# Copying a chunk's four accumulators out of PSUM first and adding them one unit later, with the weight decoding moved behind

## The chip, the cores and the metric

One core of a Trainium2 chip runs the whole kernel. The metric is the device time of one execution in microseconds, given as the median of several runs. TensorE (PE) multiplies matrices, VectorE (DVE) and ScalarE (ACT) do elementwise work, SyncE (SP) issues the transfers. TensorE writes its sums to PSUM, whose banks of 128 x 512 float32 VectorE and ScalarE read.

## The reference

Three stages follow one another, with two batches of 3008 tokens and a width of 256:

```python
scores = matmul(z, z.T) / S              # z: 3008 x 64 for each batch
x = u * matmul(maximum(scores, 0)**2, v) # v: 3008 x 256
h = x @ w_in;  y = (h - tanh(h)) @ w_out                       # 2048 wide
out = (sigmoid(y @ w_gate) * (y @ w_val)) @ w_out2             # 1536 wide
```

The weights arrive as float64 and are decoded on the chip.

## The kernel before

**Units.** The tokens are cut into twelve chunks: six for each batch, five of 512 tokens and one of 448. The work on a chunk is a row of units. In the attention of the first eleven chunks (`HalfAttention`) a unit is a pair of key tiles, and there are 12 units to a chunk. For the last chunk (`Attention`) the units are mixed with those of the first feed-forward stage (`Ffn1`), and the second stage (`Ffn2`) follows in the same list.

**A unit's steps.** `front` (line 294) lets TensorE compute the scores of two key tiles into PSUM. `mid1` (line 306) lets ScalarE apply relu (line 310) and square (line 311), and then VectorE split the result into a rounded part `ah` (line 314) and a remainder `al` (line 315, which the profile shows under the helper's line 79). `back` (line 317) multiplies both parts with the values `v` and adds to the chunk's accumulators. Each accumulator is a PSUM bank. `HalfAttention` uses all four banks at once, `acc[h][d]`: h is the half of the rows of a key tile that two matmuls side by side work on, d the half of the 256 columns. The sum over h is the result.

**Order.** The order on every engine is written out by hand in one loop (lines 527 to 555). Iteration n first runs what `todo[n]` holds, then `front` and `mid1` of unit n, then `end` of a chunk that was finished one iteration earlier (`LATE = 1`), and then `back` of unit n - 2. Each engine has one queue and takes its instructions in this order. So VectorE has from the end of a unit's scores to that unit's `back`, two iterations later, to make `ah` and `al`, and what lies ahead in its queue uses up that time.

**What todo holds.** The steps that decode the weights, six iterations for a part of 512 columns or rows (lines 133 to 178): `magnitude`, `sign`, `join`, `rest(0)`, `rest(1)`, `add` on lines 155 to 177, nearly all VectorE's; the splits of `v`, `z`, `x` and of the decoded weights; and the loads.

**A chunk's turn.** In iteration n in which `back` of a chunk's last unit is issued (unit n is then the second of the next chunk) the loop runs `todo[n]`, `front`, `back`, and then `empty` (line 339): for each d ScalarE copies `acc[1][d]` to SBUF (line 344) and VectorE adds `acc[0][d]` from PSUM to it (line 345). `mid1` of unit n comes after that. The next chunk's first `back`, one iteration later, writes the same four banks, and so can't start before they have been read. In iteration n + 1 `end` (line 347) lets VectorE multiply the sum by `u` (line 349) and SyncE write the product to memory (line 350). There are eleven such turns in a run.

**Buffers.** `mid1` and `empty` take their SBUF tiles from a ring of nine (`work`, line 67), `u`, `v`, `z` and weights from a ring of 42 (`ring`, line 66).

Of the kernel before, what the change touches and what calls it, by code (L numbers as in the profile page):

```python
# [7 lines left out]
F32 = mybir.dt.float32  # L8
# [4 lines left out]
ALU = mybir.AluOpType  # L13

P = 128
NQ = 512
# [14 lines left out]
def squared_relu_attention__then__two_ffns(  # L31
# [17 lines left out]
    nc = tc.nc  # L49
# [4 lines left out]
    ND = D // P  # L54
# [20 lines left out]
    def tmp(shape, dtype, name):  # L75
        return work.tile([P, *shape], dtype, tag="w", name=name)
# [165 lines left out]
    class Attention(Unit):  # L242
# [41 lines left out]
        def end(self, acc):  # L284
            u, n = u_t[self.c], self.n
            for d in range(ND):
                nc.vector.tensor_tensor(out=u[:, d, :n], in0=acc[d][:, :n], in1=u[:, d, :n], op=ALU.mult)
            nc.sync.dma_start(out=spill[self.c], in_=u[:, :, :n])

    class HalfAttention(Attention):  # L290
# [47 lines left out]

        def empty(self, acc):
            n = self.n  # L340
            self.sum = tmp([ND, NQ], F32, "sum")
            for d in range(ND):
                t = self.sum[:, d, :n]
                nc.scalar.copy(t, acc[1][d][:, :n])
                nc.vector.tensor_tensor(out=t, in0=acc[0][d][:, :n], in1=t, op=ALU.add)  # L345

        def end(self, acc):
            u, n = u_t[self.c], self.n
            nc.vector.tensor_tensor(out=u[:, :, :n], in0=self.sum[:, :, :n], in1=u[:, :, :n], op=ALU.mult)
            nc.sync.dma_start(out=spill[self.c], in_=u[:, :, :n])  # L350

    class Ffn1(Unit):
# [92 lines left out]
    units = [HalfAttention(c, i) for c in range(NC - 1) for i in range(KP)]  # L445
# [12 lines left out]
    todo = {}  # L458
# [5 lines left out]
    for b in range(B):  # L464
# [14 lines left out]
        for j in range(NZ):  # L479
            n = need[j] + early[j]  # L480
# [3 lines left out]
    for c in range(NC):  # L484
        at(start[0, c] + 2, lambda c=c: load_u(c))
        n = start[1, c]
# [7 lines left out]
    n = 8  # L494
    half = start[0, NZ]
    split = {}
    for k, p in enumerate(parts):
# [5 lines left out]
        if half - 14 < n < half + 4:  # L503
            n = half + 4
    for f in range(N1):
        n = where[1, 0, f]
        at(n - 3, split["wi1_", f // 2][f % 2])
        at(n - 2, split["wo1_", f // 2][f % 2])
    for f in range(N2 // 2):
        n = where[1, 0, 0] + W2_LAG + 2 * f  # L510
# [7 lines left out]
    with tc.manual_schedule():  # L518
        nc.vector.memset(square_max, -SQUARE_MAX)
        nc.scalar.activation(warm, square_max, AF.Tanh)  # L520
        accs = {}
        backs = {}
        for n, u in enumerate(units):
            backs.setdefault(n + u.ahead, []).append(u)
        pending = []
        total = len(units)
        for n in range(total + 8):
            for fn in todo.pop(n, ()):
                fn()
            if n < total:  # L530
                units[n].front()
            ready = backs.pop(n, ())

            turn = any(u.last and isinstance(u, HalfAttention) for u in ready)
            if n < total and not turn:
                units[n].mid1()
            if 0 <= n - 1 < total:
                units[n - 1].mid2()
            if pending and n >= pending[0][0]:
                _, u, a = pending.pop(0)  # L540
                u.end(a)
            for u in ready:
                halves = isinstance(u, HalfAttention)
                if u.first:
                    accs[u.kind] = [
                        [psa.tile([P, NQ], F32, tag=f"acc{d}", name=f"acc{d}") for d in range(ND)] for _ in range(1 + halves)
                    ]
                acc = accs[u.kind] if halves else accs[u.kind][0]
                u.back(acc)
                if u.last:  # L550
                    if halves:
                        u.empty(acc)
                    pending.append((n + LATE, u, acc))
            if n < total and turn:
                units[n].mid1()
        assert not todo and not pending


# [26 lines left out]
```

## Time and profile before

| | us |
|---|---|
| median of 3 runs (1593.74 to 1595.03) | 1593.95 |
| the profiled execution's own time | 1595.15 |
| its span | 1593.4 |
| TensorE busy in it | 1578.7 (99%) |
| VectorE busy | 1110.1 (70%) |
| ScalarE busy | 1044.2 (66%) |

The eleven chunks of `HalfAttention` take the first 459 us of the span, some 40 us for each. The granted clock of TensorE is 1.0, its full 2.4 GHz, in all 40 slices. In a timeline a row gives start, duration and engine, the line of the kernel, the operation with its output and inputs, the count and, in brackets, how long the engine sat idle before it and what ended that. Instructions on one engine overlap by some tenths of a microsecond, so what one of them costs its queue is read from start to start.

### The profile page before, as it was taken

What the parts mean: (1) busy time and instruction counts of PE and PEld (TensorE: products, weight loads), DVE (VectorE), ACT (ScalarE), POOL (GpSimd) and SP (SyncE); (2) the same over time, 40 slices, a digit from 0 to 9 for tenths busy, and PEclk for the clock granted to TensorE, in tenths of its full rate; (3) what the DMA queues carried; (4) which work ended last, traced back from release to release, by engine and by line L of the source; (5) the groups of instructions that cost most, each with busy time, mean ns of one, the idle gap of its engine ahead of it and who ended that gap; (6) DMA issues with size and microseconds to landing.
All of it is one profiled execution on the core that took longest, in us unless ns stands there. A gap on an engine that the chain in (4) does not pass through costs nothing.

```text
span 1593.4 us, 21476 instructions
## 1 busy us (share of the span) xinstructions
PE 1578.7 (99%) x8980; PEld 1338.8 (84%) x8980; DVE 1110.1 (70%) x1256; ACT 1044.2 (66%) x1254; POOL 0.2 (0%) x4
## 2 busy tenths in 40 slices
PE   8999999999999999999999999999999999999999
PEld 6888889888888878888888888888888888888888
DVE  7988898988879886666656656666656566665542
ACT  8766678677678986666566656566656666666532
POOL 0000000000000000000000000000000000000000
PEclk9999999999999999999999999999999999999999
DMA  6222233211100000000000000000000000000000
GB/s 225 80 80 80 74 104 100 81 67 54 52 14 14 1 25 1 27 1 1 27 1 25 0 27 1 27 0 1 26 0 27 1 27 1 0 25 1 14 1 25
DMA packets 28161, 53.28 MB, mean 33 GB/s; under 512 B 1952, under 2 KB 10144, under 8 KB 28064
## 3 DMA queue, kind: packets, MB, share of 16 engines
q1 hardware_dynamic: 28064, 51.91, 9.5%
q8 instruction: 70, 1.15, 0.3%
q14 instruction: 27, 0.22, 0.0%
HBM read 39.58 MB, written 12.32 MB: 33 GB/s over the span
## 4 chain that ended last, share of the span: by engine, by line
PE 95%; DVE 2%; ACT 1%; DMA 1%; issue 1%; SPq 0%; DVEq 0%
PE acc L223 30%; PE gv L235 24%; PE acc L331 20%; PE h L235 16%; PE s L302 5%; PE s L257 1%; DMA vraw<-v 0%; DMA raw_wg<-w_gate 0%; DVE ah L314 0%; ACT a L310 0%; DVE e L79 0%; DVE v L79 0%; ACT a L311 0%; DVE al L79 0%; DVE th L378 0%
## 5 line engine op out<-in xcount | busy, mean ns | idle before, releaser
L79 DVE TENSOR_TENSOR e<-h,th 128x1024 f32<-128x1024 f32 (+1 forms) x96 | 115.5, 1203 | 285.1 <-ACT sq L373 285.1
L331 PE MATMUL acc<-ah,v 64*128 64x512 f32 (+1 forms) x2068 | 301.1, 387 | 1.8 <-DVE sum L345 1.7
L331 PEld LDWEIGHTS acc<-ah,v 64*128 64x128 f32 x2068 | 218.1, 185 | 33.8 <-DVE sum L345 2.9
L372 ACT ACTIVATE th<-h 128x1024 f32<-128x1024 f32 (+1 forms) x96 | 97.0, 1010 | 216.3 <-PE h L235 216.3
L235 PE MATMUL h<-xh,wi 128*128 128x512 f32 (+1 forms) x768 | 233.8, 386 | 0.8 <-DVE e L79 0.8
L223 PE MATMUL acc<-p,wo 128*128 128x512 f32 (+1 forms) x864 | 215.4, 385 | 0.0
L223 PE MATMUL acc<-gh,wo 128*128 128x512 f32 (+1 forms) x768 | 204.8, 386 | 0.5 <-DVE yl L79 0.4
L310 ACT ACTIVATE a<-s 128x1024 f32<-128x1024 f32 (+1 forms) x132 | 134.2, 1017 | 87.2 <-PE s L302 85.9
L223 PEld LDWEIGHTS acc<-p,wo 128*128 128x128 f32 x864 | 162.2, 188 | 30.0
L422 ACT ACTIVATE sg<-gv 128x512 f32<-128x512 f32 (+1 forms) x144 | 84.6, 588 | 156.8 <-PE gv L235 156.8
L331 PE MATMUL acc<-al,v 64*128 64x512 f32 (+1 forms) x1034 | 184.0, 388 | 0.1
L79 DVE TENSOR_TENSOR al<-a,ah 128x1024 fp32r<-128x1024 f32 (+2 forms) x145 | 173.4, 1196 | 7.4 <-DVE ah L314 0.5
L235 PE MATMUL gv<-yh,wg 128*128 128x512 f32 (+1 forms) x576 | 175.2, 385 | 0.0
L235 PE MATMUL gv<-yh,wv 128*128 128x512 f32 (+1 forms) x576 | 175.0, 385 | 0.0
L423 DVE TENSOR_TENSOR sg<-gv,sg 128x512 f32<-128x512 f32 (+1 forms) x144 | 98.0, 680 | 106.5 <-ACT sg L422 106.5
L235 PEld LDWEIGHTS h<-xh,wi 128*128 128x128 f32 x768 | 144.1, 188 | 28.1 <-DVE e L79 1.3
L223 PEld LDWEIGHTS acc<-gh,wo 128*128 128x128 f32 x768 | 144.1, 188 | 28.1 <-DVE yl L79 1.2
L235 PE MATMUL h<-xl,wi 128*128 128x512 f32 (+1 forms) x384 | 147.9, 385 | 0.0
L311 ACT ACTIVATE a<-a 128x1024 f32<-128x1024 f32 (+1 forms) x132 | 139.0, 1053 | 4.2
L378 DVE COPY_PREDICATED th<-m,e 128x1024 f32<-128x1024 uint32 (+1 forms) x96 | 131.4, 1369 | 10.3 <-ACT wv L183 0.5
L331 PEld LDWEIGHTS acc<-al,v 64*128 64x128 f32 x1034 | 114.2, 185 | 17.7 <-DVE al L79 3.3
L235 PEld LDWEIGHTS gv<-yh,wg 128*128 128x128 f32 x576 | 108.1, 188 | 20.2
(95 smaller groups left out, 2269.6 us busy)
## 6 DMA issues: line engine op xcount, KB each, us to landing
raw_wo<-w_out SPq DMA_DIRECT2D x14, 512.0 KB, 5.4
vraw<-v SPq DMA_DIRECT2D x10, 512.0 KB, 7.1
u<-uT SPq DMA_DIRECT2D x10, 512.0 KB, 7.3
x<-u SPq DMA_DIRECT2D x10, 512.0 KB, 3.1
xl<-x SPq DMA_DIRECT2D x10, 512.0 KB, 3.6
outT<-o SPq DMA_DIRECT2D x20, 256.0 KB, 2.1
raw_wi<-w_in SPq DMA_DIRECT2D x8, 512.0 KB, 8.3
zraw<-zT SPq DMA_DIRECT2D x12, 256.0 KB, 6.7
```

The costliest lines, as they stand in the source:

```text
L79: nc.vector.tensor_tensor(out=out, in0=a, in1=b, op=ALU.subtract)
L223: nc.tensor.matmul(acc[d][:, :n], wt[:, wi, w, d * P : (d + 1) * P], hl[ai], start=first and m == 0, stop=last and m == len(passes) - 1,)
L235: nc.tensor.matmul(ps, w[:, wi, d, fi * P : (fi + 1) * P], xs[xi][:, d, :n], start=m == 0, stop=m == len(passes) - 1)
L257: nc.tensor.matmul(self.ps[:, e, :n], k, z_t[b, self.j][:, h, :n], start=h == 0, stop=h == 1)
L302: nc.tensor.matmul(self.ps[:, e, :n], z_t[b, i // 4][r, ki ^ e, c : c + P], q[r, qi ^ e, :n], start=m == 0, stop=m == 2)
L310: nc.scalar.activation(s, self.ps[:, :, :n], AF.Relu, scale=SCALE)
L311: nc.scalar.activation(s, s, AF.Square)
L331: nc.tensor.matmul(acc[h][d][:, :n], vt[r, w, e, d * P : (d + 1) * P], self.hl[a][r, e, :n], start=self.first and banks[k] not in banks[:k ...
L372: nc.scalar.activation(t, h, AF.Tanh)
L378: nc.vector.copy_predicated(t, m.bitcast(U32), e)
L422: nc.scalar.activation(s[:, :n], self.ps[:, 0, :n], AF.Sigmoid)
L423: nc.vector.tensor_tensor(out=s[:, :n], in0=self.ps[:, 1, :n], in1=s[:, :n], op=ALU.mult)
```

## The change

`empty` now reads each bank once and adds nothing: for each d VectorE copies `acc[0][d]` and ScalarE copies `acc[1][d]`, to two tiles of their own. `end`, one iteration later, lets VectorE add the two tiles, in one instruction over both d, and then multiply by `u`. In a turn's iteration `todo[n]` runs last, behind `mid1` of unit n, where it ran first.

```diff
         def empty(self, acc):
             n = self.n
-            self.sum = tmp([ND, NQ], F32, "sum")
+            self.sums = [tmp([ND, NQ], F32, "sum") for _ in range(2)]
             for d in range(ND):
-                t = self.sum[:, d, :n]
-                nc.scalar.copy(t, acc[1][d][:, :n])
-                nc.vector.tensor_tensor(out=t, in0=acc[0][d][:, :n], in1=t, op=ALU.add)
+                nc.vector.tensor_copy(self.sums[0][:, d, :n], acc[0][d][:, :n])
+                nc.scalar.copy(self.sums[1][:, d, :n], acc[1][d][:, :n])
 
         def end(self, acc):
             u, n = u_t[self.c], self.n
-            nc.vector.tensor_tensor(out=u[:, :, :n], in0=self.sum[:, :, :n], in1=u[:, :, :n], op=ALU.mult)
+            s, t = (a[:, :, :n] for a in self.sums)
+            nc.vector.tensor_tensor(out=s, in0=s, in1=t, op=ALU.add)
+            nc.vector.tensor_tensor(out=u[:, :, :n], in0=s, in1=u[:, :, :n], op=ALU.mult)
             nc.sync.dma_start(out=spill[self.c], in_=u[:, :, :n])
...
         for n in range(total + 8):
-            for fn in todo.pop(n, ()):
-                fn()
+            ready = backs.pop(n, ())
+
+            turn = any(u.last and isinstance(u, HalfAttention) for u in ready)
+            if not turn:
+                for fn in todo.pop(n, ()):
+                    fn()
             if n < total:
                 units[n].front()
...
-            if n < total and turn:
-                units[n].mid1()
+            if turn:
+                if n < total:
+                    units[n].mid1()
+                for fn in todo.pop(n, ()):
+                    fn()
```

## Rows read from the trace of the kernel before

**Rows 1.** The page's busy time, share of the span and instructions of each engine.

```profile
PE 1578.7 (99%) x8980; PEld 1338.8 (84%) x8980; DVE 1110.1 (70%) x1256; ACT 1044.2 (66%) x1254; POOL 0.2 (0%) x4
```

**Rows 2.** Waits of TensorE over the span: us in total, times, longest us.

```profile
PE acc L331 <- DVE sum L345: 1.7, 2, 1.1
```

**Rows 3.** Timeline of TensorE at turns 1 and 5 (where that wait falls).

```profile
56.64 0.73 PE L331 MATMUL acc<-ah,v 64*128 64x512 f32 x3 [0.53 <-DVE sum L345]
...
220.01 0.66 PE L331 MATMUL acc<-ah,v 64*128 64x448 f32 x3 [1.13 <-DVE sum L345]
```

**Rows 4.** Groups of instructions by shape: busy us, mean ns, idle before.

```profile
L345 DVE TENSOR_TENSOR sum<-acc,sum 128x512 f32<-128x512 f32 x20 | 13.6, 687 | 3.8 <-ACT sum L344 3.7
...
L345 DVE TENSOR_TENSOR sum<-acc,sum 128x448 f32<-128x448 f32 x2 | 1.2, 622 | 0.3 <-ACT sum L344 0.3
...
L440 DVE COPY o<-acc 128x448 f32<-128x448 f32 x1 | 0.6, 625 | 2.4 <-PE acc L223 2.4
...
L344 ACT COPY sum<-acc 128x512 f32<-128x512 f32 x20 | 11.7, 587 | 27.5 <-PE acc L331 27.5
```

**Rows 5.** Timeline of VectorE around turn 9.

```profile
374.81 1.23 DVE L79 TENSOR_TENSOR al<-a,ah 128x1024 fp32r<-128x1024 f32 x1
375.95 0.68 DVE L171 SCALAR_TENSOR_TENSOR wg_s<-raw_wg,wg_s 128x512 f32<-128x512 uint32 x1
376.56 0.68 DVE L345 TENSOR_TENSOR sum<-acc,sum 128x512 f32<-128x512 f32 x1
377.65 0.69 DVE L345 TENSOR_TENSOR sum<-acc,sum 128x512 f32<-128x512 f32 x1 [0.42 <-ACT sum L344]
379.68 0.70 DVE L314 CAST ah<-a 128x1024 fp32r<-128x1024 f32 x1 [1.33 <-ACT a L311]
380.41 1.22 DVE L79 TENSOR_TENSOR al<-a,ah 128x1024 fp32r<-128x1024 f32 x1
381.55 0.68 DVE L171 SCALAR_TENSOR_TENSOR wg_s<-raw_wg,wg_s 128x512 f32<-128x512 uint32 x1
382.15 0.69 DVE L314 CAST ah<-a 128x1024 fp32r<-128x1024 f32 x1
382.94 1.23 DVE L79 TENSOR_TENSOR al<-a,ah 128x1024 fp32r<-128x1024 f32 x1
384.09 1.22 DVE L349 TENSOR_TENSOR u<-sum,u 128x1024 f32<-128x1024 f32 x1
385.22 1.22 DVE L177 TENSOR_TENSOR wg<-wg,wg_s 128x1024 f32<-128x1024 f32 x1
386.36 0.69 DVE L314 CAST ah<-a 128x1024 fp32r<-128x1024 f32 x1
387.15 1.23 DVE L79 TENSOR_TENSOR al<-a,ah 128x1024 fp32r<-128x1024 f32 x1
```

**Rows 6.** Timeline of TensorE around turn 9: a front, then a back's two halves.

```profile
380.23 0.84 PE L302 MATMUL s<-z,z 64*128 64x512 f32 x6
...
387.71 1.07 PE L331 MATMUL acc<-ah,v 64*128 64x512 f32 x8
388.62 0.63 PE L331 MATMUL acc<-al,v 64*128 64x512 f32 x4
```

**Rows 7.** Windows: the stretch, its length, then busy us of PE, PEld, DVE, ACT.

```profile
380.00:390.00 10.00, 10.00 (x92) 8.20 (x90) 9.72 (x12) 8.88 (x10) 0.00 (x0) 1.00 0.34 117
```

**Rows 8.** Timeline behind turn 2, VectorE and TensorE.

```profile
102.18 0.69 DVE L314 CAST ah<-a 128x1024 fp32r<-128x1024 f32 x1 [0.57 <-ACT a L311]
...
106.72 1.22 DVE L79 TENSOR_TENSOR al<-a,ah 128x1024 fp32r<-128x1024 f32 x1
...
108.00 0.73 PE L331 MATMUL acc<-al,v 64*128 64x512 f32 x4
```

**Rows 9.** Timeline behind turn 11, VectorE and TensorE.

```profile
473.00 1.22 DVE L79 TENSOR_TENSOR gl<-th,gh 128x1024 fp32r<-128x1024 f32 x1
...
474.64 0.62 PE L223 MATMUL acc<-gl,wo 128*128 128x512 f32 x2
```

More of the change, by code (lines that the diff above doesn't have):

```diff
@@ L527, in squared_relu_attention__then__two_ffns @@
         for n in range(total + 8):
-            for fn in todo.pop(n, ()):
-                fn()
+            ready = backs.pop(n, ())
[3 more added lines that the diff above has]
+                    fn()
             if n < total:
                 units[n].front()
-            ready = backs.pop(n, ())
-            turn = any(u.last and isinstance(u, HalfAttention) for u in ready)
             if n < total and not turn:
```

## The prediction

> **What bounds the kernel now.** I read the page's first part, then TensorE's waits, then the places where they fall, then VectorE's queue around a chunk's turn. TensorE is busy for 99% of the span, VectorE for 70% [rows 1]. So anything that keeps TensorE waiting is added to the end, and little is there to be won. Of all of TensorE's waits those on the sums at a turn make 1.7 us, in 2 pieces [rows 2]: 0.53 at turn 1 and 1.13 at turn 5 [rows 3]. That is what the change can remove: about 0.1% of the time.
>
> The share of 70% is an average over the run. Behind a turn VectorE has no room: in the 10 us from 380.00 it is busy for 9.72 [rows 7]. Rows 5 show why, at turn 9. VectorE waits for ScalarE's square and gets `ah` of the turn's unit (call it U) only at 379.68, after 0.42 and 1.33 us of idling; ScalarE has two copies and a unit to work off first. From there on the queue stands without a gap through U, U+1, the product with `u` (384.09) and U+2: it is catching up. `ah` of U+2 starts at 386.36 and is done 0.69 later, at 387.05; its `al` starts at 387.15 and is done at 388.38. TensorE takes up the one at 387.71 and the other at 388.62 [rows 6]. So VectorE is 0.66 us early with `ah` and 0.24 us early with `al`, of which some 0.05 passes between any releaser's end and the start. Behind turn 2 the margin is used up: `al` starts at 106.72 and is done at 107.94, and TensorE starts on it at 108.00 [rows 8]. Whatever the change adds to VectorE's queue between `ah` of U and `al` of U+2 makes TensorE wait, but for that margin.
>
> **The change, part by part.** *The copies for the sums.* Each turn had two VectorE additions out of PSUM, of 0.69 us each for 512 columns, and gets two VectorE copies out of PSUM. None of 512 columns is in the trace. At 448 columns such a copy takes 625 ns and the addition 622 [rows 4], so I take 0.69; the ends are 0.63 and 0.8. It hardly matters. ScalarE's second copy takes 0.59 [rows 4] and releases the second sum at 377.65, so the bank is complete at about 377.05; both VectorE copies can be over by 377.8, and nothing follows for VectorE until 379.68. The idle time there, 1.75 us in all [rows 5], covers them. ScalarE's work is the same two copies at the same place, so `ah` of U stays at 379.68.
>
> *The wait of TensorE for the sums.* The copies no longer stand behind a weight step or ScalarE's copy. The 1.7 us go [rows 2]. What is late next is `ah` and `al`.
>
> *The weight step moved back.* It ran where VectorE then idled, waiting for ScalarE; now it stands between `al` of U and U+1, where VectorE is catching up. At turn 9 it is `rest(0)`, and costs 0.60 from start to start (375.95 to 376.56); `ah` of U+1 moves from 382.15 to 382.75. At turns 1 to 5 it is `add`, which from start to start takes 1.14 (385.22 to 386.36, another such step) [rows 5]; 0.57 of that falls into idle time that is there [rows 8], so that 0.5 to 0.6 is left. At turn 6 it is the split of a `v` tile, at turn 11 that of a weight, one VectorE instruction over 512 columns as `rest` is. No held step at any of the eleven turns issues a transfer: the loads fall into other iterations.
>
> *The addition in `end`.* New on VectorE: 128 x 1024 from SBUF. The product on the same shape takes 1.22 and lets the next instruction start 1.13 after it [rows 5]. The product now needs the sum's result, so it waits for the whole 1.22, and I take 1.24. The ends are 1.13 and 1.3. A gain is excluded: no instruction goes for it. It stands behind `al` of U+1 and ahead of `ah` of U+2.
>
> *Sum at turn 9.* `ah` of U+2: 386.36 + 0.60 - 0.07 + 1.24 = 388.13 (the 0.07 since `ah` to `al` took 0.79 in U+1 and takes 0.73 when nothing else is late, as in U). It ends at 388.82, and TensorE, due at 387.71, starts at about 388.87. `al` follows at 388.86, is done at 390.09, and TensorE, due at 388.62, starts at 390.14: 1.5 us lost. Later units are not late further, since TensorE's delay moves their due times too; VectorE finds its idle time again late in the chunk, but that returns nothing to TensorE. At turn 2: 0.5 to 0.6 and 1.24, less the margin of 0.06: 1.6 to 1.8, of which I take 1.6, for VectorE's queue is free a little ahead of the end of its last instruction. At turn 11, among longer units: 0.6 and 1.24, and `gl` done at 474.22 where TensorE takes it up at 474.64 [rows 9], a margin of 0.4: 1.4.
>
> *All turns.* Turns 1 to 5 as turn 2: 8.0. Turn 6 and turns 7 to 10 as turn 9: 7.5. Turn 11: 1.4. Together 16.9, less the 1.7 that go: **15.2 us slower**. The profiled execution, 1595.15, becomes 1610.4. It stands 1.2 above the median, and so the median of 1593.95 becomes 1609.1.
>
> *At nothing.* The second SBUF tile from the ring of nine: `al` of U+1 then takes a tile that `back` of unit U-1, the next chunk's first, still reads. That `back` is through when the next front starts at 380.23 [rows 6], well before `al` of U+1 is due at 383.48; were that cover gone, it would be the same lateness again, not a new one. The store in `end` leaves SyncE's queue some 1.8 us later, and loads of weights stand behind it; they are asked for six units before their use, which is the cover.
>
> A rule of the Trainium skill stands against this sum. Rows 7 show VectorE at 9.72 of 10 us just where the addition goes. The Trainium skill, Perfetto Trace Analysis, section Optimizing Scalar/DVE Operations, says that where VectorE is not saturated but causes bubbles on another engine, breaking up instructions may let work be done sooner. By its whole-run share VectorE is not saturated, and the change does break up the sum; by that the added work is free, and the time would be 1592.3. By the rows it is saturated in that stretch, and the sum is 1609.1.
>
> **The rivals.**
>
> *Hidden.* VectorE's idle time takes the additional work, and only the 1.7 us go: 1593.95 - 1.7 = 1592.3, within 0.2% of before, which is about what a measurement of this kernel can tell from no change (3.2 us). For it: VectorE idles 30% of the span [rows 1], and two iterations lie between `mid1` and `back`. Against it: the margins of 0.06 and 0.24 us [rows 5, 6, 8]. It decides if `al` of U+2 has over 1.8 us to spare behind most turns. Chance 0.09; with a little more won at turns 1 and 5 it would just reach a measurable gain, 0.03.
>
> *Only the addition counts.* The held step finds room, so each turn costs 1.24 less 0.1 to 0.2 of margin: 11 x 1.1 - 1.7 = 10.4, or 1604.4. For it: the idle time of 0.57 at turn 2. Against it: no idling at turn 9 between 379.68 and 387.15. Chance 0.12.
>
> *A load behind the store.* SyncE's store waits for the product, and a weight load behind it comes late; VectorE's `sign` or `rest` would wait for it with `ah` behind them. At 0.6 us more for each of ten turns: 1615. Against it: six units of cover. Chance 0.05.
>
> *The change doesn't do what it says.* The next chunk's first `back` still waits, since VectorE's copies stand behind a late `al` of U-1: the 1.7 stay, 1610.8. Chance 0.04.
>
> **How the numbers follow.** The forecast as worked out has 0.67. From 1601 to 1614 lie the forecast, the second and the fourth rival, and the ends of the prices: at 1.2 us a turn 1605, at 1.8 without margin and with all eleven turns alike 1593.95 + 19.8 = 1613.8; 1601 allows for a few turns with more margin than those that I walked through. Slower by over 0.2%: 0.88. Within 0.2%: 0.09. Faster: 0.03.
>
> **What would show it.** Right: at turns 1 and 5 TensorE no longer waits for a sum or a copy; new waits of TensorE on `ah` and `al`, of about 1 us and a few tenths, once behind each turn, in the third unit after it; the chunks from turn to turn some 1.5 us longer each; the feed-forward stages unchanged in length. VectorE's idle time just ahead of `ah` of U is longer, about 1.9 us. Wrong: chunks of the same length, with VectorE's gaps late in the chunk shorter by the 1.2 us; or waits of VectorE on a transfer.

## The result and the profile after

The changed kernel takes 1610.6 us (median of 5 runs, 1610.1 to 1610.88) against 1593.95: a ratio of 1.0103, 95% interval 1.009 to 1.0117. It is 16.65 us slower; 15.2 was forecast. The time alone doesn't tell the forecast from the fourth rival, which gave 1610.8 with the waits on the sums still there; the waits do, below.

The page's first part of the changed kernel answers to [rows 1]:

```profile
PE 1584.8 (99%) x8980; PEld 1319.6 (82%) x8980; DVE 1123.2 (70%) x1267; ACT 1044.0 (65%) x1254; POOL 0.2 (0%) x4
```

VectorE has eleven instructions and 13.1 us more, one addition for each turn. Its share is still 70%: the average doesn't show what happened. TensorE's waits do (us in total, times, longest); of the wait of 1.7 us on the sums [rows 2] nothing is left, and these are new or have grown:

```profile
PE acc L331 <- DVE ah L314: 9.7, 12, 1.2
...
PE acc L223 <- DVE gl L79: 1.0, 1, 1.0
```

Where the time lies is read from turn to turn. The table has the start of ScalarE's first copy (line 344) at each turn, taken from the timelines, as the distance to the next turn; the last column is from turn 11 to the end of the span.

| us from turn | 1 | 2 | 3 | 4 | 5 | 6 | 7 | 8 | 9 | 10 | 11 to end |
|---|---|---|---|---|---|---|---|---|---|---|---|
| before | 41.15 | 40.59 | 40.61 | 40.50 | 37.74 | 40.60 | 40.46 | 40.13 | 40.14 | 41.24 | 1136.12 |
| after | 42.28 | 42.29 | 42.26 | 42.18 | 39.07 | 42.21 | 41.81 | 41.82 | 41.85 | 42.92 | 1137.17 |
| longer by | 1.13 | 1.70 | 1.65 | 1.68 | 1.33 | 1.61 | 1.35 | 1.69 | 1.71 | 1.68 | 1.05 |
| forecast | 1.07 | 1.6 | 1.6 | 1.6 | 0.47 | 1.5 | 1.5 | 1.5 | 1.5 | 1.5 | 1.4 |

The differences add up to 16.6 us, the difference of the medians. (The two spans themselves differ by 14.9, because in the profiled execution of the changed kernel the first turn came at 52.44 rather than 54.12. Over all profiles of this study it comes between 52.44 and 54.20.)

VectorE's timeline at turn 9 of the changed kernel, to be laid beside [rows 5]:

```profile
385.26 1.23 DVE L79 TENSOR_TENSOR al<-a,ah 128x1024 fp32r<-128x1024 f32 x1
386.57 0.69 DVE L343 COPY sum<-acc 128x512 f32<-128x512 f32 x1
387.48 0.69 DVE L343 COPY sum<-acc 128x512 f32<-128x512 f32 x1 [0.21 <-PE acc L331]
390.16 0.70 DVE L314 CAST ah<-a 128x1024 fp32r<-128x1024 f32 x1 [1.99 <-ACT a L311]
390.89 1.23 DVE L79 TENSOR_TENSOR al<-a,ah 128x1024 fp32r<-128x1024 f32 x1
392.03 1.28 DVE L171 SCALAR_TENSOR_TENSOR wg_s<-raw_wg,wg_s 128x512 f32<-128x512 uint32 x2
393.24 0.69 DVE L314 CAST ah<-a 128x1024 fp32r<-128x1024 f32 x1
393.96 1.23 DVE L79 TENSOR_TENSOR al<-a,ah 128x1024 fp32r<-128x1024 f32 x1
395.10 1.22 DVE L349 TENSOR_TENSOR sum<-sum 128x1024 f32<-128x1024 f32 x1
396.35 1.22 DVE L350 TENSOR_TENSOR u<-sum,u 128x1024 f32<-128x1024 f32 x1
397.49 1.22 DVE L177 TENSOR_TENSOR wg<-wg,wg_s 128x1024 f32<-128x1024 f32 x1
398.63 0.69 DVE L314 CAST ah<-a 128x1024 fp32r<-128x1024 f32 x1
399.35 1.23 DVE L79 TENSOR_TENSOR al<-a,ah 128x1024 fp32r<-128x1024 f32 x1
```

The copies take 0.69 us and end in the gap ahead of `ah` of the turn's unit U (390.16), which has grown to 1.99 us. Then the queue stands without a gap: two weight steps in one row at 392.03 where one stood before, the addition at 395.10, the product 1.25 later. `ah` of U+2 starts 13.37 us after the `al` of the first row; 11.55 lay between them before (386.36 - 374.81), and the forecast's sum gave 13.32. TensorE's timeline at the same place, beside [rows 6] and the front that stood ahead of that back before, at 387.03:

```profile
387.03 0.84 PE L302 MATMUL s<-z,z 64*128 64x512 f32 x6
```

After:

```profile
397.52 0.84 PE L302 MATMUL s<-z,z 64*128 64x512 f32 x6
399.37 1.19 PE L331 MATMUL acc<-ah,v 64*128 64x512 f32 x8 [1.01 <-DVE ah L314]
400.63 0.74 PE L331 MATMUL acc<-al,v 64*128 64x512 f32 x4
401.21 1.09 PE L331 MATMUL acc<-ah,v 64*128 64x512 f32 x8
```

The wait for `ah` is in the open, 1.01 us. But from the front to the first back group 1.85 us pass rather than the 0.68 of other units: 1.17 us lost, of which 1.01 shows as a wait, since the matmuls ahead are shown as busy to their modelled ends. From there to the `al` group 1.26 pass rather than the 0.91 of [rows 6]: 0.35 more, without a wait in brackets. So the 9.7 us of waits are a part of the 16.6 only.

At eight turns (1 to 4 and 7 to 10) the wait falls as here, in the third unit behind the turn. Turn 5 differs, and the rows of before show why: there `todo` holds two instructions for VectorE, the split of a `v` tile and an `add`, and the change puts both behind `al` of U. First before, then after:

```profile
217.53 0.69 DVE L79 TENSOR_TENSOR v<-vraw,v 128x512 fp32r<-128x512 f32 x1
218.13 1.22 DVE L177 TENSOR_TENSOR wg<-wg,wg_s 128x1024 f32<-128x1024 f32 x1
219.27 1.28 DVE L345 TENSOR_TENSOR sum<-acc,sum 128x512 f32<-128x512 f32 x2
...
226.71 0.69 DVE L79 TENSOR_TENSOR v<-vraw,v 128x512 fp32r<-128x512 f32 x1
227.31 1.22 DVE L177 TENSOR_TENSOR wg<-wg,wg_s 128x1024 f32<-128x1024 f32 x1
228.55 1.39 DVE L79 TENSOR_TENSOR z<-zraw,z 64x512 fp32r<-64x512 f32 x2
229.86 0.61 DVE L314 CAST ah<-a 128x896 fp32r<-128x896 f32 x1
...
230.53 1.08 PE L331 MATMUL acc<-ah,v 64*128 64x448 f32 x8 [1.18 <-DVE ah L314]
```

From start to start the two take 1.84 us (226.71 to 228.55). `ah` of U+1 is late by them, ahead of the addition, and TensorE waits one unit sooner. At turn 6 the loss comes in pieces over several units: the one wait on `ah` there, 0.50 at 284.11, falls three units later than at the other turns.

### The profile page after: what moved, and what is told of

The parts are those of the page before. It is cut to its first block, busy times and chain, and to the rows that moved or that the text cites. A ratio compares the mean times of both kernels' runs of the same rounds, so it can differ in the third digit from the quotient of the medians.

```text
span 1608.3 us, 21461 instructions
## 1 busy us (share of the span) xinstructions
PE 1584.8 (99%) x8980; PEld 1319.6 (82%) x8980; DVE 1123.2 (70%) x1267; ACT 1044.0 (65%) x1254; POOL 0.2 (0%) x4
## 3 DMA queue, kind: packets, MB, share of 16 engines
q8 instruction: 70, 1.15, 0.3%
## 4 chain that ended last, share of the span: by engine, by line
PE 88%; DVE 7%; issue 3%; ACT 2%; DMA 1%; SPq 0%; DVEq 0%
PE acc L223 29%; PE gv L235 24%; PE h L235 15%; PE acc L331 15%; PE s L302 3%; DVE ah L314 1%; DVE al L79 1%; ACT a L311 1%; ACT a L310 1%; DVE sum L349 1%; PE s L257 1%; DMA raw_wg<-w_gate 0%; DMA vraw<-v 0%; DVE wi L177 0%; DVE e L79 0%
## 5 line engine op out<-in xcount | busy, mean ns | idle before, releaser
L331 PE MATMUL acc<-ah,v 64*128 64x512 f32 (+1 forms) x2068 | 286.3, 387 | 9.7 <-DVE ah L314 9.7
L331 PEld LDWEIGHTS acc<-ah,v 64*128 64x128 f32 x2068 | 194.4, 185 | 53.3 <-DVE ah L314 15.6
L331 PE MATMUL acc<-al,v 64*128 64x512 f32 (+1 forms) x1034 | 168.1, 390 | 1.1
L235 PEld LDWEIGHTS gv<-yh,wv 128*128 128x128 f32 x576 | 108.1, 188 | 20.2
```

What stands on the lines that cost most here:

```text
L235: nc.tensor.matmul(ps, w[:, wi, d, fi * P : (fi + 1) * P], xs[xi][:, d, :n], start=m == 0, stop=m == len(passes) - 1)
L331: nc.tensor.matmul(acc[h][d][:, :n], vt[r, w, e, d * P : (d + 1) * P], self.hl[a][r, e, :n], start=self.first and banks[k] not in banks[:k ...
```

## The experiments

Each kernel was timed in four to eleven runs beside the kernel before, whose median was then 1594.1 to 1594.7; "slower by" is against that median. Where the turns are given, they are distances between turns as in the table above.

**One part alone: the copies and the late addition.** The loop of the kernel before, with `empty` and `end` of the changed one:

```diff
-            if not turn:
-                for fn in todo.pop(n, ()):
-                    fn()
+            for fn in todo.pop(n, ()):
+                fn()
...
-            if turn:
-                if n < total:
-                    units[n].mid1()
-                for fn in todo.pop(n, ()):
-                    fn()
+            if n < total and turn:
+                units[n].mid1()
```

> The copies at the turn and the addition in `end` stay; the weight steps go back to the head of the turn's iteration. Theory (VectorE's queue behind the turn's unit has no room, so what is added to it there reaches TensorE less a margin of 0.06 to 0.24 us): each turn loses the addition, 1.24 us less the margin, about 1.0, and the waits at turns 1 and 5 stay: 1604, between 1602 and 1606. Rival (it is the steps held back that cost, and the addition finds room): 1594 to 1595.

Measured: 1604.26 us, ratio 1.0060 (1.0048 to 1.0073), slower by 9.6, as the theory had it in the sum. The turns 2 to 4 and 8 to 10 are 1.1 us longer than before, but turn 1 only 0.57 and turn 5 not at all. At those two TensorE still waits for the banks, now for the copies behind the weight step (0.54 and 1.12):

```profile
PE acc L331 <- DVE sum L343: 1.7, 2, 1.1
```

While TensorE is held there, VectorE catches up by as much, and the addition costs less by the wait: 0.57 at turn 1, where 1.15 less 0.54 is 0.61, and nothing at turn 5. So a wait at the turn and the work put behind it don't add up. TensorE's timeline at turn 9 of this kernel:

```profile
393.54 1.20 PE L331 MATMUL acc<-ah,v 64*128 64x512 f32 x8 [0.43 <-DVE ah L314]
394.80 0.73 PE L331 MATMUL acc<-al,v 64*128 64x512 f32 x4
```

The same wait at the same place, 0.58 shorter than in the changed kernel: about the weight step of 0.60 that isn't held back here.

**The other part alone: the steps held back.** The loop of the changed kernel, with `empty` and `end` of the kernel before:

```diff
-            for fn in todo.pop(n, ()):
-                fn()
+            if not turn:
+                for fn in todo.pop(n, ()):
+                    fn()
...
-            if n < total and turn:
-                units[n].mid1()
+            if turn:
+                if n < total:
+                    units[n].mid1()
+                for fn in todo.pop(n, ()):
+                    fn()
```

> The sum stays at the turn as before, in two VectorE additions out of PSUM; only the weight steps of the turn's iteration are held back behind `mid1`. Theory: each turn loses 0.3 to 0.5 us (a step of 0.60, or one of 1.14 of which 0.57 falls into idle time, less the margin), and the waits of 1.7 us at turns 1 and 5 go: 1597.4, between 1595.5 and 1599. Rival (the held steps are the cost): 1608 or more.

Measured: 1599.06 us, ratio 1.0028 (1.0017 to 1.0039), slower by 4.4, a little above the expected band. Of the waits on sums nothing is left, but TensorE gets a new one on `ah`:

```profile
PE acc L331 <- DVE ah L314: 1.3, 2, 1.2
```

At turn 1 the wait that went was won: the distance is 0.09 shorter, where a held step makes about 0.5 at other turns. At turn 5 the distance grew by 0.80 though the wait of 1.13 in it had gone: the two steps held there cost 1.93, and the 1.2 above is TensorE's wait for `ah` of U+1 behind them. At turn 11 the held step costs nothing. The two parts alone make 9.6 + 4.4 = 14.0; together they make 16.6. By turns, the rest is 0.65 and 0.53 at turns 1 and 5, 0.41 and 0.37 at turns 7 and 11, and 0.02 to 0.09 at each of the others. At turns 1 and 5 it is the wait, which covers the addition in part or in whole when the copies stand alone and is gone here; at turn 5 the lateness of the held steps then covers a part of it. At turns 7 and 11 VectorE had a little room that each part alone uses up and the two together have only once: the margin of 0.4 that the forecast read at turn 11, and at turn 7 of the kernel before an idling of 0.46 ahead of `al` of U+1:

```profile
302.70 1.23 DVE L79 TENSOR_TENSOR al<-a,ah 128x1024 fp32r<-128x1024 f32 x1 [0.46 <-DVE ah L314]
```

**The suspected cost doubled.** One more VectorE instruction of the same shape in `end`:

```diff
+            nc.vector.tensor_tensor(out=s, in0=s, in1=s, op=ALU.max)
             nc.vector.tensor_tensor(out=s, in0=s, in1=t, op=ALU.add)
```

> The changed kernel with one more VectorE instruction of the same shape (128 x 1024) ahead of the addition in `end`, which leaves the tile as it is. Theory: no margin is left, so each of eleven turns loses the whole 1.24 us more: 13 us above the changed kernel, 1623.5, between 1621 and 1625.5. Rival (TensorE's loss comes from a new wait elsewhere, such as ScalarE's for a tile of the ring, and the addition itself is partly hidden): under 1617.

Measured: 1633.91 us, ratio 1.0247 (1.0233 to 1.0261): 23 us above the changed kernel where 13 were expected, and outside the expected band. Against the changed kernel the distances from turns 5, 6 and 7 grew by 1.24, 1.16 and 1.25, as expected, and those from turns 1 to 4 and 8 to 10 by 2.1 to 2.5. The timelines of TensorE and the windows (stretch, length, busy us of PE, PEld, DVE, ACT, POOL, then the granted clock) tell why. First turn 7, then turn 9:

```profile
328.56 1.20 PE L331 MATMUL acc<-ah,v 64*128 64x512 f32 x8 [2.29 <-DVE ah L314]
329.82 0.73 PE L331 MATMUL acc<-al,v 64*128 64x512 f32 x4
...
330.00:332.00 2.00, 2.00 (x20) 1.62 (x21) 1.90 (x3) 0.00 (x0) 0.00 (x0) 1.00 1.03 378
...
415.91 2.05 PE L331 MATMUL acc<-ah,v 64*128 64x512 f32 x8 [2.26 <-DVE ah L314]
417.75 1.06 PE L331 MATMUL acc<-al,v 64*128 64x512 f32 x4
...
416.00:418.00 2.00, 2.00 (x10) 1.63 (x12) 2.00 (x3) 1.06 (x1) 0.00 (x0) 0.50 0.96 275
```

At both turns TensorE had sat idle for about 2.3 us. At turn 7 the granted clock is 1.00; at turn 9 it is 0.50 behind the wait, the lower level of 1.2 GHz, and ten matmuls run in the two microseconds that hold twenty at turn 7. So each turn pays the 1.24 us of the instruction, which bears the theory out, and behind eight of the eleven (all but 5 to 7) comes a stretch at the lower clock, which neither theory had. Behind turn 11 no wait of 2.3 us stands ahead of it but two short ones close together, of 0.86 (509.06) and 1.05 (511.30). What sets turn 7 apart from turn 9 is not shown. In the changed kernel itself, with waits of about 1 us, the clock is 1.00 throughout; none of its loss is of this kind.

**The same work, elsewhere in the queue.** `end` of these chunks six units behind the turn, with the two tiles in a place of their own:

```diff
-    ring = ctx.enter_context(tc.tile_pool(name="ring", bufs=42))
-    work = ctx.enter_context(tc.tile_pool(name="work", bufs=9))
+    ring = ctx.enter_context(tc.tile_pool(name="ring", bufs=41))
+    work = ctx.enter_context(tc.tile_pool(name="work", bufs=8))
+    late = ctx.enter_context(tc.tile_pool(name="late", bufs=2))
...
-            self.sums = [tmp([ND, NQ], F32, "sum") for _ in range(2)]
+            self.sums = [late.tile([P, ND, NQ], F32, tag="sum", name="sum") for _ in range(2)]
...
-                    pending.append((n + LATE, u, acc))
+                    pending.append((n + (6 if halves else LATE), u, acc))
```

> The changed kernel with `end` (addition, product and store) six units behind the turn rather than one, where VectorE has idle time again; the two tiles get a place of their own, for which the ring of nine has eight tiles and the ring of 42 has 41. Same instructions on every engine. Theory: VectorE's queue behind the turn loses the addition and the product, so most of the loss goes: 1594 to 1597. Rival (VectorE has too much work in the attention as a whole, and the addition costs wherever it stands): 1604 or more.

Measured: 1598.53 us, ratio 1.0021 (1.0012 to 1.0030), slower by 3.8, just above the band. The addition is as long and as frequent as in the changed kernel, and nearly 13 of the 16.6 us are gone. The product moves with it, so VectorE's queue behind the turn is also freer than in the kernel before, which had the product there. From turns 1 to 3 the distances are shorter than before by 0.7, 0.1 and 0.2, from 8 to 10 the same as before. What is left lies at turns 4 to 7, around the change of batches (0.4, 0.4, 1.6 and 0.6 longer; at turn 6 VectorE's queue has no gap from 267.94 to 296, and waits on the copies come back at two turns, 0.9 us in all), and behind turn 11 (1.9), where the late addition now meets the first feed-forward units:

```profile
PE acc L224 <- DVE gl L80: 1.5, 1, 1.5
```

So it isn't the amount of VectorE's work that costs but its place: two units behind a turn there is no room, late in a chunk there is, and where there is none late in the chunk either it costs there.

**ScalarE's new waits.** The changed kernel has waits that the forecast did not have. ScalarE's timeline at turn 9:

```profile
396.41 1.03 ACT L310 ACTIVATE a<-s 128x1024 f32<-128x1024 f32 x1 [1.14 <-DVE sum L349]
...
400.67 1.03 ACT L310 ACTIVATE a<-s 128x1024 f32<-128x1024 f32 x1 [2.14 <-DVE al L79]
```

The relu of later units waits for tiles of the ring of nine, first for one that the addition gives back. Over the run that is 14.3 us for the addition and 15.2 for `al`. The edit gives the ring eleven tiles:

```diff
-    ring = ctx.enter_context(tc.tile_pool(name="ring", bufs=42))
-    work = ctx.enter_context(tc.tile_pool(name="work", bufs=9))
+    ring = ctx.enter_context(tc.tile_pool(name="ring", bufs=40))
+    work = ctx.enter_context(tc.tile_pool(name="work", bufs=11))
```

> The changed kernel with eleven tiles in the ring that had nine, for which the ring of 42 has 40: ScalarE's new waits for a tile that the late addition or a late `al` gives back (14.3 and 15.2 us in the changed kernel's profile) should go or shrink. Theory: they cost nothing, since VectorE's queue behind is later still: 1610.6, between 1609 and 1612. Rival (ScalarE's lateness is part of TensorE's waits on `ah`): 1607 or less.

Measured: 1612.92 us, ratio 1.0116 (1.0101 to 1.0132): no faster, and 2 us above the changed kernel rather than level with it. Both of ScalarE's waits are gone from the profile, and TensorE's on `ah` is what it was:

```profile
PE acc L331 <- DVE ah L314: 9.7, 12, 1.2
```

The distances from turn to turn are within 0.2 us of the changed kernel's; from turn 11 to the end it is 0.8 longer. So ScalarE's waits are covered: VectorE would not have come to that unit's `ah` earlier. Where the additional 2 us come from (two tiles fewer in the other ring, for one) was not tried.

**The addition and the product on GpSimd.** In the changed kernel, `nc.gpsimd` for `nc.vector` on both lines of `end`:

```diff
-            nc.vector.tensor_tensor(out=s, in0=s, in1=t, op=ALU.add)
-            nc.vector.tensor_tensor(out=u[:, :, :n], in0=s, in1=u[:, :, :n], op=ALU.mult)
+            nc.gpsimd.tensor_tensor(out=s, in0=s, in1=t, op=ALU.add)
+            nc.gpsimd.tensor_tensor(out=u[:, :, :n], in0=s, in1=u[:, :, :n], op=ALU.mult)
```

> The changed kernel with both instructions of `end` (addition and product) on GpSimd, which does nothing else. Theory: VectorE's queue loses 2.4 us behind each turn against the changed kernel, and the steps held back alone remain, without the product that stood there before: 1593 to 1596. Rival (GpSimd working beside VectorE makes VectorE slower, or its late product holds a tile that ScalarE needs): 1600 or more.

Measured: 1628.92 us, ratio 1.0215 (1.0201 to 1.0229): slower by 34, and the rival was right. The timelines at turn 9 of this kernel, VectorE, GpSimd and TensorE:

```profile
402.29 1.11 DVE L314 CAST ah<-a 128x1024 fp32r<-128x1024 f32 x1 [1.98 <-ACT a L311]
403.43 3.28 DVE L79 TENSOR_TENSOR al<-a,ah 128x1024 fp32r<-128x1024 f32 x1
406.63 1.28 DVE L171 SCALAR_TENSOR_TENSOR wg_s<-raw_wg,wg_s 128x512 f32<-128x512 uint32 x2
...
400.44 2.40 POOL L349 TENSOR_TENSOR sum<-sum 128x1024 f32<-128x1024 f32 x1 [39.08 <-DVE sum L343]
402.92 2.70 POOL L350 TENSOR_TENSOR u<-sum,u 128x1024 f32<-128x1024 f32 x1
...
406.76 0.73 PE L331 MATMUL acc<-al,v 64*128 64x512 f32 x4 [2.12 <-DVE al L79]
```

While GpSimd multiplies, from 402.92 to 405.62, VectorE's `al` takes 3.28 us in place of 1.23, and TensorE waits for it for 2.12. `al` ends at 406.71, 1.09 us behind the product's end, about as if it had begun only then. The Trainium skill, Perfetto Trace Analysis, section Optimizing Scalar/DVE Operations, says that GpSimd and VectorE share an SBUF read port, so that moving work from the one to the other might not help. The trace agrees that it doesn't help, with 2.05 us more on one VectorE instruction; that the port is the reason, no run here shows. The 34 us are not the price of this alone: behind turns 2 to 5 and 8 to 10 a stretch at the lower clock follows, as in the kernel with the addition doubled. At turn 9:

```profile
409.00:411.00 2.00, 2.00 (x14) 1.53 (x12) 2.00 (x3) 0.23 (x1) 0.00 (x0) 0.50 0.98 339
```

Turns 1 and 7 have the same wait of 2.12 at a clock of 1.00 and are 1.9 and 2.2 us longer than before, turns 8 to 10 4.1.

**The kernel before with its product on GpSimd.**

```diff
-            nc.vector.tensor_tensor(out=u[:, :, :n], in0=self.sum[:, :, :n], in1=u[:, :, :n], op=ALU.mult)
+            nc.gpsimd.tensor_tensor(out=u[:, :, :n], in0=self.sum[:, :, :n], in1=u[:, :, :n], op=ALU.mult)
```

> The kernel before with only the product of `end` on GpSimd. Theory: VectorE's queue behind a turn gets 1.14 us shorter, and the few tenths that TensorE lost there go: about 1 us faster than before, 1592.5 to 1594.5, less than can be told from no change. Rival (GpSimd's work makes VectorE slower): 1598 or more.

Measured: 1601.42 us, ratio 1.0042 (1.0029 to 1.0054), slower by 6.8. Again the rival. The timelines of VectorE and GpSimd at turn 9 of this kernel:

```profile
384.50 1.75 DVE L314 CAST ah<-a 128x1024 fp32r<-128x1024 f32 x1 [1.33 <-ACT a L311]
...
383.30 2.40 POOL L349 TENSOR_TENSOR u<-sum,u 128x1024 f32<-128x1024 f32 x1 [38.80 <-DVE sum L345]
```

`ah` of U takes 1.75 us beside the product on GpSimd, and 0.70 at the same place in [rows 5].

**The weight step in the gap.** In the changed kernel, `todo` between the copies and `mid1` rather than behind it:

```diff
             if turn:
-                if n < total:
-                    units[n].mid1()
                 for fn in todo.pop(n, ()):
                     fn()
+                if n < total:
+                    units[n].mid1()
```

> The changed kernel with the weight step between the copies and `mid1` of the turn's unit, where VectorE sits idle for 1.99 us waiting for ScalarE's square. Theory: the step is hidden there (0.60 or 1.14 us), so only the addition is left, and TensorE's wait for the sums stays away: 1600 to 1604, at or a little below the kernel with the copies alone (1604.3). Rival (the steps cost the same wherever they stand in the turn's iteration): 1609 or more.

Measured: 1604.94 us, ratio 1.0071 (1.0058 to 1.0083): 5.7 us faster than the changed kernel, about level with the copies alone (slower by 10.8 against 9.6), and a little above the expected band. VectorE's timeline at turn 9 of this kernel, and TensorE's wait behind it:

```profile
383.96 0.69 DVE L343 COPY sum<-acc 128x512 f32<-128x512 f32 x1 [0.21 <-PE acc L331]
384.57 0.68 DVE L171 SCALAR_TENSOR_TENSOR wg_s<-raw_wg,wg_s 128x512 f32<-128x512 uint32 x1
386.64 0.70 DVE L314 CAST ah<-a 128x1024 fp32r<-128x1024 f32 x1 [1.39 <-ACT a L311]
...
395.25 1.19 PE L331 MATMUL acc<-ah,v 64*128 64x512 f32 x8 [0.40 <-DVE ah L314]
```

At turn 9 the step costs nothing in the gap, and 1.39 us of it are left over. TensorE's wait for the copies is gone here, but that wins nothing: turn 1 is 0.56 us longer than before and turn 5 0.17, against 0.57 and 0 with the wait in the kernel with the copies alone. At turn 1 TensorE waits 0.60 for `ah` instead, in the third unit behind the turn. The addition itself in the gap was not tried.

**The same place for the step in the kernel before**, with the sum still at the turn: the loop of the experiment above, `empty` and `end` of the kernel before.

```diff
-            for fn in todo.pop(n, ()):
-                fn()
+            if not turn:
+                for fn in todo.pop(n, ()):
+                    fn()
...
+            if turn:
+                for fn in todo.pop(n, ()):
+                    fn()
+                if n < total:
+                    units[n].mid1()
-            if n < total and turn:
-                units[n].mid1()
```

> The kernel before with the same place for the weight step: behind the sum, ahead of `mid1`; the sum stays at the turn. Theory: nothing is added to VectorE's queue behind the turn's unit, and the sum no longer stands behind the step: the wait of 1.7 us goes, 1592 to 1594, the fastest of all, though hardly more than can be told from no change. Rival (at turns 1 and 5 TensorE only waits for `ah` or `al` a little later instead, and at turns 5, 6 and 11 the step's ScalarE part delays the unit): 1594 to 1596.

Measured: 1593.51 us, ratio 0.9997 (0.9988 to 1.0006). TensorE's wait for the sums is gone from the profile, and from turns 1 and 5 the distances are 0.55 and 0.86 us shorter than before; from turn 6 it is 0.50 longer. So with no work added behind them, most of the 1.7 us of waits can be had. In the sum that is under 1 us, which can't be told from no change. It has the lowest median of all the kernels here, but it isn't shown to beat the kernel before.

## Why the prediction was right

- **The bound.** TensorE's path sets the time, and VectorE's queue in the three units behind a turn sets TensorE's path there. That carried the whole forecast, and the experiments bear it out from three sides: work added there costs (the two parts alone, the addition doubled), the same work six units later mostly doesn't, and a step moved into the gap ahead of `ah` of U mostly doesn't.
- **The copies at nothing.** Right: 0.69 us each, over before the gap ends.
- **The addition.** 1.24 were taken; from its start to the product's it is 1.25 (395.10 to 396.35). Alone it makes 1.1 us at turns 2 to 4 and 8 to 10, the price less the margin.
- **The held step.** 0.60 at turn 9 was right to 0.02. Alone it makes about 0.5 at turns 1 to 4, 6 and 8 to 10, 0.2 at turn 7 and nothing at turn 11. At turn 5 it is the mis-sized term: the prediction has `add` alone there ("At turns 1 to 5 it is `add`"), 0.5 to 0.6, but the rows of before show the split of a `v` tile beside it, and the two together cost 1.93.
- **Turn by turn.** Ten of the eleven turns came within 0.35 us of the forecast. Turn 6 did so by another way than the forecast's, which had it as turn 9: its 1.61 is spread over several units, and so its number is in part luck. Turns 8 to 10 lost 0.2 more than worked out: 0.35 at the `al` group was foreseen, the 0.13 at the group behind it (401.21, where 401.08 was due) was not.
- **The 1.7 us that go.** The waits on sums did go, which excludes the fourth rival. At turn 1 the forecast with this taken off came out (1.13 against 1.07). At turn 5 the loss was 1.33 rather than 0.47, and the wait is not the reason: 0.86 of its 1.13 is won where nothing is held. TensorE waits there for `ah` of U+1, by 1.18, behind the two held steps; its wait behind the addition, in the next unit, is then only 0.42.
- **Turn 11** lost 1.05 rather than 1.4, a wait of 1.03 on `gl`.
- **The ring at nothing.** Right in its price, wrong in its reason: the ring did make ScalarE wait, for 29.5 us in all, and that was covered by VectorE's lateness, as eleven tiles showed.
- **The skill's rule.** By the Trainium skill, Perfetto Trace Analysis, section Optimizing Scalar/DVE Operations, breaking up the sum could have let the work be done sooner, as VectorE isn't saturated. The banks were read sooner (at turn 9 the last was read 1.8 us after the start of ScalarE's first copy rather than 2.4), and the wait for them went. The runs side with the rows of the stretch, not with the share of the run: VectorE was full where the second half of the broken-up sum was put.

## What to carry to other kernels

An engine that is busy 70% of the time can have no room at all just where work is moved to. Read what stands there at every place that the edit touches: ten turns that fitted said nothing of the one where two steps were held. Before an instruction is put off, look for the first gap behind it in that engine's queue and for what is due before that gap; here the put-off addition fell among the instructions that TensorE was waiting for, while 1.4 us stood idle one step ahead. And a wait that is taken away on the fast path is worth only what the next lateness behind it leaves: at turn 1 it was worth 0.55 us with nothing added behind it, and nothing with the addition there.

## What was not expected of the hardware

- Waits of 2.3 us on TensorE, in the kernel with the addition doubled, were followed at most turns by a stretch at a granted clock of 0.50 (1.2 GHz), and those turns grew by 0.9 to 1.3 us more than the others; the same wait at turn 7 was not, and behind turn 11 two waits of 0.86 and 1.05 close together were. With the addition and the product on GpSimd, waits of 2.1 were followed by such a stretch at turns 2 to 5 and 8 to 10 and not at turns 1 and 7. In the changed kernel, with waits of about 1 us, the clock stayed at 1.00.
- A GpSimd instruction over 128 x 1024 took 2.4 to 2.7 us where VectorE's takes 1.22, and a VectorE subtraction beside it 3.28 rather than 1.23. The product alone on GpSimd, eleven times in the run, made the kernel before 6.8 us slower.
